# One pool of eight PSUM banks, four-bank score visits in segment 0, an exponential read from SBUF, and a new order

## The chip, the cores and the metric

The kernel runs on one core of one Trainium2 chip. The metric is the device time of one execution in microseconds. The core has TensorE (PE, with its weight loads shown as PEld), VectorE (DVE), ScalarE (ACT), GpSimd (POOL) and SyncE (SP), which here issues every DMA. PSUM has eight banks of 128 partitions by 512 fp32 values; matmuls write there, and DVE and ACT read it.

## The reference

A pre-norm layer on 2048 tokens of width 640: attention with a compressive memory, then a feed-forward network. Both halves are followed by a residual add.

```
h  = x + attention(layernorm(x))
h2 = h + feedforward(layernorm(h))

attention, 32 heads of width 20, 4 segments of 512 tokens, for each segment s:
    p      = softmax(causal(q k' / sqrt(20)));   a_dot = p v
    a_mem  = (phi(q) M) / (phi(q) z + 1e-6)      phi(t) = t + 1 if t > 0 else exp(t)
    o      = g a_mem + (1 - g) a_dot             g = sigmoid(beta), one per head
    M     += phi(k)' v;   z += sum phi(k)
    output = o wo
feedforward: silu(h w1) w2, inner width 1728
```

M and z start at zero, so segment 0 has no memory term.

## The kernel before, in words

The work is cut into named tasks (some 1,380), each with an engine, the tiles it reads and writes, and the code that emits its instructions. A string, `ORDER`, lists all tasks in one fixed order, found by a search outside the kernel with a model of costs. Each engine executes its own tasks in the order in which they stand there; between engines, semaphores that a tracker derives from reads and writes make an instruction wait. An entry such as `oe6x/A:0` names the task, for tasks that two engines can do the one chosen (A for ACT, D for DVE), and the buffer slots it takes. The numbers given to `G.task` as costs and priorities were of use to the search; in the emitted program only the order, the slots and the choice of engine count.

Names of tasks, with segment or tick numbers behind them:

- `n1_st`, `n1_rs`, `n1_ap`, `n1_tp`, `n1_te`, `n1_tr`: layernorm of a block of 128 tokens (statistics on DVE, root on POOL, apply on DVE) and its transpose, by matmul with an evacuation for segment 0 and by DMA afterwards. `n2_` is the same before the feed-forward network.
- `v`, `ve`: V projection (ten matmuls, L776) and its evacuation into Vx. `pr`: projection of q (last digit 0) or k (1) for a chunk of heads (five matmuls, L804); `qe`: the cast of its bank to QK (ACT L814 or DVE L815); `ex`: exp of it for phi (ACT L820); `ph`: the rest of phi on DVE (L827, L830). `re_`: rearrangement of the weights wq and wk.
- `qk`: a score visit, matmuls for a group of four heads (L877). The four heads are four row tiles of TensorE that write four banks. `e`: exp of two of those banks (ACT L888); `mk`: causal mask on POOL (L900).
- `av`: p v with four column tiles (L923); `oe`: evacuation into oTs (ACT L936, DVE L938); `tn`: transposes of it and the memory product (L952, L956); `nm`: division (DVE L969 to L989); `ad`: sum of both parts on POOL (L997).
- `kt`, `mz`, `ma`, `mb`: transpose of phi(k) by DMA, its product with V, and the update of Mz and its masked copy. `vt`: small DMAs that gather the heads 20 to 31 into QKV.
- `ot`, `wo`, `rs`: transpose of the attention's output by DMA (L1097), its product with wo (L1105), the residual add. `h1`, `th`, `s`: product with w1 (L1129), tanh on ACT (L1137), silu on DVE (L1143). `h2`, `o`, `out`: product with w2 (L1160), residual add (L1170), store.
- `w_...`, `x...`, `beta`: loads. The loads of wo, w1, w2 and the later x wait for a certain `nm` of segment 0. `fill31`: 31 matmuls on zeros into a free bank, whose result nobody reads.

Segment 0 has its groups in two halves of the queries: a tick x for the first 256 (score set `x`, 384 columns) and a tick y for the rest (sets `ya` of 512 columns and `yb` of 384). The segments 1 to 3 have one tick per group with sets `a`, `b` and, shared by two groups, `e`.

PSUM is two tensors of four banks: `ps_gen`, whose banks go to everything but scores (pool `ps`), and `ps_sc` for scores (pool `sc`). In segment 0 a score set is made in two visits of two banks each, in the other segments in one visit of four (`QUAD_SEGS`). An `ex` reads the projection's bank, as the `qe` does; reads of one bank by two engines are kept apart by the tracker, one behind the other.

The order interleaves the segments: while segment s is in its ticks, the projections of s + 1 and the feed-forward network of s - 1 are placed between the score visits. Behind the last score visit stand the last wo, h1 and h2 products.

Of the kernel before, what the change touches and what calls it, by code (L numbers as in the profile page):

```python
# [8 lines left out]
F32 = mybir.dt.float32  # L9
# [35 lines left out]
class Tracker:  # L45
# [29 lines left out]
    @staticmethod  # L75
    def _is_exclusive(key):
        return key[0] in ("ps", "sc")
# [133 lines left out]
class Alloc:  # L211
# [10 lines left out]
    def keys(self, subs):  # L222
        if self.pool in ("ps", "sc"):
            return [(self.pool, self.slot + i) for i in range(self.size)]
        return [(self.pool, self.slot, s) for s in subs]
# [99 lines left out]
D = 640  # L325
# [20 lines left out]
QUAD_SEGS = (1, 2, 3)  # L346
# [24 lines left out]
pr101:1 nm6x:0 e4ya0:1 e3yb2:1 av1y:0 oe0y/D:1 qk2yb0:2 e2yb0:0 qk2yb2:0 e2yb2 ex101:2 v12:2 qk3yb0:2 kt04:0 mta2
ot1:0 mm5 mk2yb ot0 w_w1_0 w_w1_2 e3yb0 w_w1_4 w_w1_1 oe1y/D:0 qe101/D:0 ph031:0 ve12/D qk2ya0:0 e2ya0:0 wo1:0 rs1
qk4ya2:2 qk2ya2:0 e2ya2 wo0:2 e4ya2 n2_st1:0 av2y:0 qk3ya0:0 e3ya0:0 qk3ya2:2 e3ya2 rs0 n2_st0:2 tn1y:1 pr120:2
qk4yb0:0 oe2y/D:0 tn2y:0 e4yb0:0 tn0y:3 qk4yb2:2 nm1y:0 n2_rs1 mk3yb mta0 mtb0 mm3 av3y:1 n2_rs0 e4yb2 n2_ap1:1
mk4yb nm0y:0 nm2y:1 qk5yb0:0 n2_ap0:0 qe120/D:0 mz00:3 mz04:0 ma00/D:1 e5yb0:1 oe3y/D:1 ph101:1 qk5ya2:2 ma04/D:2
ex120:0 e5ya2:0 qk5ya0:0 pr111:3 n2_tr1:0 qk5yb2:2 av4y:2 e5ya0 n2_tr0 qk6yb2:0 tn3y:0 h1_0_7_0:1 qe111/D:0 oe4y/D:0
tn4y:2 e5yb2 e6yb2:0 nm3y:1 ex111:2 nm4y:1 kt03:0 qk6ya0:2 x8:8,9,10,11 kt02:1 qk6yb0:0 ph111:0 ph120:0 h1_0_1_0:0
pr100:3 e6ya0:1 mk5yb mm6 e6yb0 mk6yb th0_7_0:0 ex100:0 qk6ya2:2 qk7yb0:0 e6ya2 qe100/D av5y:2 e7yb0:1 s0_7_0:0
h1_0_6_0:3 av6y:1 qk7ya0:2 oe5y/D:0 ph100:0 th0_1_0:0 th0_6_0:1 n1_st9:2 qk7yb2:0 e7yb2 e7ya0:1 s0_6_0 oe6y/D:1
s0_1_0 pr110:2 qk7ya2:0 tn6y:3 pr130:1 n1_st10:0 e7ya2 tn5y:0 nm6y:1 qk8a0:0 pr121:3 qe130/D:0 nm5y:1 ex110:0  # L380
ex130:2 e8a0:0 qe110/D e8a2 mz02:0 h1_0_11_0:1 th0_11_0:0 ex121:1 n1_st11:1 h1_0_5_0:2 th0_5_0:1 ma02/D:3 qe121/D
ph110:0 s0_11_0 vt16:0 w_w2_0:0 qk8b0:0 e8b2:0 e8b0 mm9 mzc3 mtb2 mzc9 mm4 mzc4 n1_rs9 mk7yb av7y:0 oe7y/D:0 mk8b
mm2 mm10 mm0 mzc6 s0_5_0 pr131:3 kt10:1 n1_st8:3 ex131:0 h1_0_2_0:1 tn7y:0 qk8e0:0 nm7y:1 th0_2_0:1 pr141:2 s0_2_0
h1_0_4_0:0 qe131/D h1_0_3_0:1 ph121:2 e8e0:1 e8e2 qk9a0:0 th0_4_0:1 th0_3_0:0 ot2 ot3 e9a2:1 e9a0 s0_4_0 ex141:1 mm7
n1_rs8 mm1 mzc1 mzc2 mzc10 mk8e mk8a mzc0 mzc5 n1_rs11 mz03:3 mm8 mb01:0 n1_rs10 mb00:0 mm11 mzc8 s0_3_0 h1_0_10_0:0
pr140:1 th0_10_0:0 ph130:0 qe141/D:0 ma03/D:4 qk9b0:0 wo2:2 n1_ap8:0 s0_10_0 e9b0:1 e9b2 av8:0 qe140/D n1_ap9:1 rs2
oe8/D:0 qk10a0:0 ex140:2 wo3:2 n2_st2:2 n1_ap10:2 e10a2:0 e10a0 h1_0_8_0:0 rs3 th0_8_0:0 qk10b0:0 e10b0:0 e10b2
# [24 lines left out]
ma22 tn19:2 nm19:1,0 e20b2:1 h2_2_2 mk20e e20b0 qk21a0:0 mk20b out3 n2_tr7 n2_tr6 e21a0:1 h2_2_3 e21a2 mk21a
h1_1_7_0:2 o2 ph240:0 mz14:3 th1_7_0:1 qk21b0:0 ma14 av20:0 out1 kt20:0 out2 x12 e21b0:0 e21b2 s1_7_0:0 oe20/D:1
# [38 lines left out]
def build(nc, es, A_x, A_wq, A_wk, A_wv, A_wo, A_beta, B_x, B_w1, B_w2, out):  # L452
# [118 lines left out]
    for b in range(4):  # L571
        load_x(b, 1, -100 + b)
# [660 lines left out]
```

## Time and profile before

| | us |
|---|---|
| median of three runs (330.74 to 332.19) | 331.64 |
| the profiled execution, its time | 331.8 |
| its span from first to last instruction | 330.1 |
| PE busy | 307.5 |
| PEld busy | 166.9 |
| DVE busy | 230.8 |
| ACT busy | 219.6 |
| POOL busy | 144.6 |

Busy time is the time in which an engine has at least one instruction in work; a matmul counts as busy for its whole way through the array, so short groups look longer than their columns. A view by stretches of time gives for each engine the busy time and, in brackets, the number of instructions, then the granted clock of TensorE (1.00 is full), the share of the DMA engines and GB/s. A row of the waits reads: who waited, for whom, us in total, times, the longest. A row of the timeline reads: start, duration, engine, line, operation, shapes, and in square brackets the idle time before it and what ended it. A row of the groups ends with the busy time and mean duration in ns, then the idle time before it.

### The profile page before, as it was taken

How to read it: one execution, taken by the hardware profiler on the slowest of the kernel's cores; microseconds unless marked ns; L12 is line 12 of the kernel's file. 1: busy time of each engine (PE TensorE's matmuls, PEld its weight loads, DVE VectorE, ACT ScalarE, POOL GpSimd, SP SyncE). 2: the span in 40 equal slices, each digit the busy share in tenths (PEclk: the TensorE clock that was granted, in tenths of full speed). 3: DMA queues.
4: the chain of work that ended last, by engine and by line, in shares of the span. 5: the costliest groups of instructions: out<-in, count | busy, mean ns of one | idle time of the engine just before them, and what ended most of it. 6: DMA issues, size and time to landing. Idle time of an engine off the chain costs nothing.

```text
span 330.1 us, 7228 instructions
## 1 busy us (share of the span) xinstructions
PE 307.5 (93%) x2874; PEld 166.9 (51%) x2874; DVE 230.8 (70%) x504; ACT 219.6 (67%) x306; POOL 144.6 (44%) x282
## 2 busy tenths in 40 slices
PE   8789798988897889998999999999999999999996
PEld 6534354444464544454654445545564446554563
DVE  5696847988898975876877985448866674855512
ACT  2659777998988798767776967776678880004400
POOL 3353861552958725273575434623576332120000
PEclk9999899999999999999999999999999999999999
DMA  7704376441744440006325030213441001350012
GB/s 209 251 0 76 71 200 180 131 97 16 165 85 86 114 108 2 1 23 107 68 66 133 24 71 10 18 33 68 93 91 34 0 2 21 60 119 2 0 40 101
DMA packets 48353, 24.56 MB, mean 74 GB/s; under 512 B 38848, under 2 KB 47232, under 8 KB 48320
## 3 DMA queue, kind: packets, MB, share of 16 engines
q1 hardware_dynamic: 48320, 24.10, 31.3%
q8 instruction: 23, 0.38, 0.5%
q14 instruction: 10, 0.08, 0.1%
HBM read 10.33 MB, written 2.62 MB: 39 GB/s over the span
## 4 chain that ended last, share of the span: by engine, by line
PE 56%; DVE 23%; ACT 7%; DMA 5%; SPq 5%; issue 3%; POOL 1%; DVEq 0%; ACTq 0%
PE ps_gen L1160 18%; PE ps_gen L1129 13%; PE ps_gen L804 6%; PE ps_sc L877 4%; PE ps_gen L923 4%; DVE stt L708 4%; PE ps_gen L1105 4%; DMA x_tok<-in_A_x_dram 4%; PE ps_gen L776 3%; DVE on L989 3%; DVE QK L815 2%; SPq L841 2%; ACT PTA L888 2%; ACT ex L820 2%; PE ps_gen L952 2%
## 5 line engine op out<-in xcount | busy, mean ns | idle before, releaser
L888 ACT ACTIVATE PTA<-ps_sc 128x1024 bf16<-128x1024 f32 x64 | 62.9, 1025 | 13.4 <-PE ps_sc L877 12.4
L1129 PE MATMUL ps_gen<-hT,w_sb 128*128 128x512 bf16 (+3 forms) x350 | 68.4, 338 | 2.5 <-DVE Vx L787 0.7
L900 POOL TENSOR_SCALAR_AFFINE_SELECT PTB<-PTB 128x512 bf16<-128x512 bf16 x64 | 40.9, 639 | 68.0 <-ACT PTB L888 65.8
L1160 PE MATMUL ps_gen<-w_sb,sT 128*128 128x320 bf16 x448 | 67.3, 300 | 0.6 <-DVE QK L815 0.2
L888 ACT ACTIVATE PTB<-ps_sc 128x1024 bf16<-128x1024 f32 (+1 forms) x64 | 59.9, 978 | 8.0 <-PE ps_sc L877 6.4
L1137 ACT ACTIVATE th<-ps_gen 128x512 f32<-128x512 f32 (+3 forms) x70 | 35.1, 520 | 39.6 <-PE ps_gen L1129 34.4
L1160 PEld LDWEIGHTS ps_gen<-w_sb,sT 128*128 128x128 bf16 x448 | 40.5, 98 | 24.1 <-issue 7.2
L1143 DVE SCALAR_TENSOR_TENSOR sT<-th,ps_gen 128x512 bf16<-128x512 f32 (+3 forms) x70 | 38.7, 570 | 16.4 <-ACT th L1137 15.9
L1129 PEld LDWEIGHTS ps_gen<-hT,w_sb 128*128 128x128 bf16 (+1 forms) x350 | 31.4, 98 | 31.7 <-issue 3.0
L888 ACT ACTIVATE PTE<-ps_sc 128x1024 bf16<-128x1024 f32 (+1 forms) x40 | 35.7, 938 | 6.3 <-PE ps_sc L877 5.2
L900 POOL TENSOR_SCALAR_AFFINE_SELECT PTE<-PTE 128x512 bf16<-128x512 bf16 x40 | 26.1, 651 | 14.3 <-ACT PTE L888 12.9
L708 DVE BATCH_NORM_STATS2 stt<-x_tok 128x6 f32<-128x320 bf16 x64 | 28.0, 480 | 3.1 <-DMA x_tok<-in_A_x_dram 3.0
L815 DVE CAST QK<-ps_gen 128x512 bf16<-128x512 f32 x31 | 21.0, 684 | 12.6 <-ACT ex L820 7.1
L1170 DVE SCALAR_TENSOR_TENSOR x_tok<-ps_gen,x_tok 128x640 bf16<-128x640 f32 x16 | 13.2, 824 | 23.2 <-PE ps_gen L1160 23.2
L776 PE MATMUL ps_gen<-wv_sb,xT 128*128 128x320 bf16 x160 | 25.3, 308 | 2.4 <-DMA wv_sb<-in_A_wv_dram 1.4
L1105 PE MATMUL ps_gen<-wo_sb,oT 128*128 128x320 bf16 x160 | 23.9, 299 | 3.5 <-DVE Mz L1070 1.2
L877 PE MATMUL ps_sc<-QK 20*128 20x256 bf16 (+3 forms) x360 | 24.1, 285 | 2.2 <-DVE QK L815 1.0
L938 DVE TENSOR_SCALAR oTs<-ps_gen,lsc 128x512 bf16<-128x512 f32 (+1 forms) x34 | 21.3, 628 | 6.8 <-PE ps_gen L923 6.8
L804 PE MATMUL ps_gen<-xT,wkr 128*128 128x512 bf16 x100 | 24.4, 380 | 1.2 <-DVE QK L815 0.6
L804 PE MATMUL ps_gen<-xT,wqr 128*128 128x512 bf16 x100 | 24.6, 380 | 0.8 <-DVE QK L815 0.8
L820 ACT ACTIVATE ex<-ps_gen 128x512 bf16<-128x512 f32 x30 | 18.1, 606 | 9.4 <-DVE QK L815 7.1
L900 POOL TENSOR_SCALAR_AFFINE_SELECT PTA<-PTA 128x512 bf16<-128x512 bf16 x24 | 15.6, 652 | 15.1 <-ACT PTA L888 15.1
(77 smaller groups left out, 401.3 us busy)
## 6 DMA issues: line engine op xcount, KB each, us to landing
out_dram<-x_tok SPq DMA_DIRECT2D x16, 160.0 KB, 2.0
w_sb<-in_B_w_dram SPq DMA_DIRECT2D x5, 432.0 KB, 5.9
x_tok<-in_A_x_dram SPq DMA_DIRECT2D x3, 640.0 KB, 4.8
w_sb<-in_B_w_dram SPq DMA_DIRECT2D x3, 640.0 KB, 5.0
QKV<-QK SPq DMA_DIRECT2D x16, 72.0 KB
wv_sb<-in_A_wv_dram SPq DMA_DIRECT2D x1, 800.0 KB, 6.9
sT<-in_A_wq_dram SPq DMA_DIRECT2D x1, 800.0 KB, 8.5
sT<-in_A_wk_dram SPq DMA_DIRECT2D x1, 800.0 KB, 10.3
```

What stands on the lines that cost most here:

```text
L708: T.add(DV, lambda e, hh=hh: e.bn_stats(out=stt[:, s, 6 * hh:6 * hh + 6], in_=xb[:, 320 * hh:320 * hh + 320]), reads=R((xa, xsub)), writes ...
L776: fns.append(lambda e, c=c, hh=hh: e.matmul(bank(ps, hh)[:, 0:320], lhsT=xT[:, c, 128 * i:128 * i + 128], rhs=wv_sb[:, c, 320 * hh:320 * h ...
L804: fns = [lambda e, kc=kc: e.matmul(bank(ps), lhsT=wt[:, kc, c, :], rhs=xT[:, kc, :], start=(kc == 0), stop=(kc == NC - 1)) for kc in range ...
L815: (lambda e: e.tensor_copy(out=o, in_=bank(ps)))
L877: fns.append(lambda e, j=j, o=o, r=r, q0=q0, q1=q1, qa=qa, ka=ka: e.matmul(sc_all[:, o:o + q1 - q0], lhsT=ka[32 * r:32 * r + DH, 128 * j:1 ...
L888: T.add(AC, lambda e: e.activation(out=pt[:, pta.slot, q0:q0 + 2, 0:width], in_=sc3[:, b0:b0 + 2, 0:width], func=ACT.Exp, scale=SCALE), re ...
L900: fns.append(lambda e, v=v: e.affine_select(out=v, in_=v, pattern=[[0, 4], [1, 128]], compare_op=ALU.is_ge, fill=0.0, base=0, channel_mult ...
L1105: fns.append(lambda e, c=c, hh=hh: e.matmul(bank(ps, hh)[:, 0:320], lhsT=oT[:, c, 128 * i:128 * i + 128], rhs=wo_sb[:, c, 320 * hh:320 * h ...
L1129: fns = [lambda e, c=c: e.matmul(bank(ps)[0:fw, lo:hi], lhsT=w1_sb[:, c, 128 * f:128 * f + fw], rhs=hT[:, c, lo:hi], start=(c == 0), stop= ...
L1137: T.add(AC, lambda e: e.activation(out=th[0:fw, tha.slot, lo:hi], in_=bank(ps)[0:fw, lo:hi], func=ACT.Tanh, scale=0.5), reads=R((ps, [0])) ...
L1143: T.add(DV, lambda e: e.scalar_tensor_tensor(out=sT[0:fw, f, lo:hi], in0=th[0:fw, tha.slot, lo:hi], scalar=1.0, in1=bank(ps)[0:fw, lo:hi], ...
L1160: fns.append(lambda e, f=f, fw=fw, hh=hh: e.matmul(bank(ps, hh)[:, 0:320], lhsT=sT[0:fw, f, 128 * i:128 * i + 128], rhs=w2_sb[0:fw, f, 320 ...
```

## The change

- One PSUM tensor of eight banks and one pool `ps` of eight slots serve everything, scores too. A score visit takes four neighbouring free banks.
- `QUAD_SEGS` includes segment 0: a set is one visit of eight matmuls and four banks, with two exps behind it as before. The 24 tasks for the second halves disappear.
- `ex` reads the bf16 cast in QK, not the bank, so it depends on the `qe` and no longer holds the bank.
- The `vt` copies of a segment use two semaphores instead of one.
- `ORDER` is new from the first entry to the last, with other slots and other choices of engine: of 40 `oe`, 15 are on ACT (6 before), of 40 `qe` 12 (9), of 16 `ve` 8 (6), of four `n1_te` 3 (2), of the five `ma` of segment 0 3 (0), of ten `re_` 4 (5). At the start 54 warm-up matmuls stand in one place, where 31 and 5 stood, and four and two more stand later, where two times two stood in segment 0.
- Several costs for the search are changed.

```diff
-        return key[0] in ("ps", "sc")
+        return key[0] == "ps"
...
-QUAD_SEGS = (1, 2, 3)
+QUAD_SEGS = (0, 1, 2, 3)
...
 ORDER = """
-zpad:0 x0:0 mt0 mt1 mt3 mta3 iota halfc epsc x1:1 x3:2 sel n1_st0:0 w_wv:0 n1_st1:1 n1_rs0 n1_ap0:0 fill31:0
-n1_tp0:0 n1_rs1 n1_ap1:1 x2:3 fill5:2 n1_tp1:2 n1_te0/A:0 n1_st3:0 n1_rs3 n1_st2:1 n1_te1/A epsg0 n1_rs2 w_q:0 v00:0
-n1_ap3:1 v01:2 ve00/A:0 n1_ap2:0 w_k n1_tp3:0 ve01/A re_wq0/A:0 n1_tp2:2 n1_te3/D v03:0 n1_te2/D pr000:2 re_wq2/A
...
+zpad:0 iota sel epsc x0:0 vpad0 mt2 x2:1 n1_st0:0 x1:2 x3:3 w_q:0 n1_st2:2 mta2 halfc mt0 mt1 n1_rs0 n1_st1:1
+n1_st3:3 epsg0 n1_ap0:0 n1_rs2 fill54:0 n1_tp0:0 n1_te0/A:0 n1_rs1 n1_rs3 n1_ap1:1 n1_ap2:2 n1_tp1:2 n1_te1/A
+n1_ap3:0 re_wq0/D:0 n1_tp2:4 n1_te2/D n1_tp3:6 n1_te3/A beta pr000:4 w_k zf0 re_wq1/A pr010:6 lsc0 re_wk0/D:0
+re_wk2/A pr001:5 re_wk1/D lsc1 mta1 lsc2 re_wk3/A qe000/D:0 pr011:7 w_wv:0 x4:4,5,6,7 qe001/A qe011/A:0 ex011:0 lsc3
+re_wq4/D re_wq2/D pr020:5 qk0x0:0 e0x2:0 e0x0 qe010/D pr031:7 pr021:6 qk1x0:0 vpad1 mtb1 mm5 mm1 mk0x n1_st5:3
...
+e7x0:0 mz02:4 e7x2 ma02/A:2 mk6x av6x:6 qk2yb0:0 mta0 mk7x e2yb2:1 e2yb0 mk2yb mtb0 tn5x:5 pr101:4 w_w2_1:0 w_w1_0:0
+w_wo:0 oe6x/D:1 av7x:6 nm5x:1 av1y:7 w_w1_3 oe7x/D:0 qk2ya0:0 ex100:1 tn6x:6 qe101/D e2ya2:0 e2ya0 nm6x:1 ex101:0
+pr130:5 tn7x:6 pr110:4 nm7x:1 qk3ya0:0 pr111:6 qe110/A:0 ph100:0 ph101:0 pr121:4 oe1y/D:0 ot0:0 qe111/D e3ya2:1
+e3ya0 qk3yb0:0 e3yb0:0 wo0:6 qe130/D:0 e3yb2 qe121/D:0 ex110:0 rs0 w_w1_1 ot1 mm0 mzc0 av2y:4 oe2y/A:1 n2_st0:3
...
+s2_11_0 h2_11_1 h2_8_0:4 h2_8_1 th2_13_0:1 ad31 s2_10_0 s2_13_0 ad30 ot15:0 wo15:0 rs15 ot14 n2_st15:2 wo14:2 ot12
...
-        "sT": 1, "th": 2, "st": 8, "const": 1, "ps": 4, "sc": 4,
+        "sT": 1, "th": 2, "st": 8, "const": 1, "ps": 8,
...
-    ps_all = es.enter_context(nc.psum_tensor("ps_gen", [128, 4 * 512], F32))
-    sc_all = es.enter_context(nc.psum_tensor("ps_sc", [128, 4 * 512], F32))
-    sc3 = sc_all[:, :].rearrange("p (b x) -> p b x", b=4)
+    ps_all = es.enter_context(nc.psum_tensor("ps_all", [128, 8 * 512], F32))
+    sc3 = ps_all[:, :].rearrange("p (b x) -> p b x", b=8)
...
-                    def e_ex(eng, ps=ps, exa=exa):
-                        T.add(AC, lambda e: e.activation(out=ex[:, exa.slot, :], in_=bank(ps), func=ACT.Exp),
-                              reads=R((ps, [0])), writes=R((exa, [0])))
+                    def e_ex(eng, c=c, w=w, exa=exa):
+                        T.add(AC, lambda e: e.activation(out=ex[:, exa.slot, :], in_=QK[:, c, w, :], func=ACT.Exp),
+                              reads=R((qk[c], [w])), writes=R((exa, [0])))
...
-        lane_v = T.lane(f"virt{s}")
+        lane_v = [T.lane(f"virt{s}a"), T.lane(f"virt{s}b")]
...
-                sca = G.alloc("sc", nr)
+                sca = G.alloc("ps", nr)
```

More of the change, by code (lines that the diff above doesn't have):

```diff
@@ L222, in keys @@
     def keys(self, subs):
-        if self.pool in ("ps", "sc"):
+        if self.pool == "ps":
             return [(self.pool, self.slot + i) for i in range(self.size)]
@@ L371 @@
[L371 to L375, printed above, removed]
```

208 lines of the change are left out of this document (102 added, 106 removed).

## The prediction

> **What bounds the kernel now.** I read the page first, then the busy time of each engine by stage, then the waits of ScalarE (ACT), then the timeline around single score visits. The page's engine totals:
>
> ```profile
> span 330.1 us, 7228 instructions
> PE 307.5 (93%) x2874; PEld 166.9 (51%) x2874; DVE 230.8 (70%) x504; ACT 219.6 (67%) x306; POOL 144.6 (44%) x282
> ```
>
> TensorE (PE) is busy for 93% of the span, VectorE (DVE) for 70%. An average hides where the rest lies, so the second view cuts the span at the first score visit, at the end of segment 0, and so on. A row has the stretch and its length in us, then the busy time (and instructions) of PE, PE's weight loads, DVE, ACT and POOL, the granted clock, and DMA:
>
> ```profile
> 0.00:18.50 18.50, 15.00 (x101) 10.00 (x101) 11.86 (x35) 8.61 (x18) 5.88 (x24) 1.00 0.64 205
> 18.50:78.60 60.10, 54.21 (x595) 26.83 (x595) 46.65 (x125) 49.19 (x73) 30.76 (x65) 0.97 0.42 104
> 78.60:150.00 71.40, 64.71 (x694) 35.73 (x694) 58.08 (x122) 60.26 (x85) 42.27 (x81) 1.00 0.33 72
> 150.00:205.00 55.00, 52.79 (x518) 28.14 (x515) 43.13 (x93) 41.86 (x55) 28.37 (x50) 1.00 0.34 69
> 205.00:272.00 67.00, 66.27 (x612) 34.34 (x610) 43.32 (x86) 51.15 (x65) 31.87 (x52) 1.00 0.22 42
> 272.00:330.00 58.00, 54.54 (x367) 31.89 (x364) 27.72 (x48) 8.57 (x15) 5.40 (x11) 1.00 0.19 49
> ...
> 60.00:90.00 30.00, 26.43 (x295) 14.24 (x293) 25.79 (x73) 27.98 (x43) 16.62 (x45) 1.00 0.41 88
> 90.00:120.00 30.00, 26.62 (x323) 15.71 (x326) 27.75 (x59) 25.06 (x35) 20.34 (x36) 1.00 0.51 113
> ```
>
> From 205 us on TensorE has nothing left to give: 66.27 of 67.00 us. Its idle time lies before: 5.9, 6.7 and 2.2 us in the three stages from 18.5 to 205 us, 14.8 us together, and 3.5 us in the startup. The last two rows say why: from 60 to 90 us ACT is busy 27.98 of 30 us, from 90 to 120 us DVE 27.75 of 30. There TensorE waits for whichever of the two is full, while the other has 2 to 5 us spare. So time comes back only if matmul slots are saved, if banks come free earlier, or if ACT and DVE are loaded more evenly before 205 us.
>
> **The change, part by part.**
>
> Four-bank visits in segment 0. Its 24 score sets are now made in one visit of eight matmuls, not two of four; matmuls, columns and exponentials are the same. A two-bank visit and a four-bank one in the timeline, each with the row after it:
>
> ```profile
> 59.69 0.34 PE L877 MATMUL ps_sc<-QK 20*128 20x256 bf16 x4
> 59.96 0.22 PE L956 MATMUL ps_gen<-ident,oTs 128*128 128x96 bf16 x1
> ...
> 78.59 0.40 PE L877 MATMUL ps_sc<-QK 20*128 20x384 bf16 x8 [0.32 <-ACT PTA L888]
> 78.92 0.29 PE L923 MATMUL ps_gen<-PTA,Vx 128*32 128x256 bf16 x4
> ```
>
> From start to next start the small visit takes 0.27 us and the large one 0.33. A set goes from 0.54 to 0.33 us, and 24 sets save 5.0 us of matmul slots. All lie in a stage where TensorE is idle 10% of the time and ACT is nearly as full, so I count half: **-2.5 us** (0 to -5.0).
>
> The other side of it: two small visits let TensorE fill one pair of banks while ACT empties the other. A large visit holds four, and in the new order the next one nearly always uses the same four, so ACT stands between them unless other work is queued there. ACT's waits, first in segment 0 (18 to 78 us), then in the rest (78 to 272 us), where the visits already are large:
>
> ```profile
> ACT PTA L888 <- PE ps_sc L877: 2.8, 6, 1.4
> ACT PTB L888 <- PE ps_sc L877: 2.7, 4, 1.6
> ACT PTE L888 <- PE ps_sc L877: 0.3, 1, 0.3
> ...
> ACT PTA L888 <- PE ps_sc L877: 9.6, 11, 1.4
> ACT PTE L888 <- PE ps_sc L877: 4.9, 7, 2.0
> ACT PTB L888 <- PE ps_sc L877: 3.7, 8, 0.7
> ```
>
> That is 5.8 us in segment 0 now. The 60 large visits later cost 18.2 us, 0.30 each; 24 of them would cost 7.2, 1.4 more. ACT is busy 49.19 of 60.10 us (0.82) in this stage, so I take 0.82 x 1.4 = **+1.1 us** (0 to +8.0; the upper end is the second rival).
>
> Exponential of the feature map from SBUF. Today the cast of q or k (DVE or ACT) and the exponential (ACT) both read the projection's bank, one after the other, and the bank is free only after both. Who waited for the exponential, and what it costs beside ACT's reads of SBUF at line 689:
>
> ```profile
>   DVE QK L815: 7.1, 8
>   PE ps_gen L1105: 0.8, 1
>   PEld ps_gen L1129: 0.8, 2
>   PEld ps_gen L804: 0.5, 1
>   PE ps_gen L804: 0.3, 1
> ...
> L820 ACT ACTIVATE ex<-ps_gen 128x512 bf16<-128x512 f32 x30 | 18.1, 606 | 9.4 <-DVE QK L815 7.1 <-DVE phiK L830 1.4 <-PE ps_gen L804 0.5
> L689 ACT ACTIVATE wkr<-sT 128x400 bf16<-128x400 bf16 x3 | 1.6, 525 | 0.0
> L689 ACT ACTIVATE wkr<-sT 128x80 bf16<-128x80 bf16 x2 | 0.5, 258 | 0.0
> ```
>
> DVE no longer waits for it (7.1 us). TensorE's own waits on it are 2.4 us with the weight loads, 1.1 without; I take **-1.5 us** (0 to -2.4). The exponential must now follow the cast in every case, where ACT could go first before: it already waits 7.1 us for casts, and the next user, the phi pair on DVE, comes much later in the order, so I cost this at nothing; without that cover it is one cast of 0.7 us per late pair. As to its duration, 80 to 400 elements from SBUF give 0.834 ns per element, so 512 take 618 ns against 606 from PSUM: 30 x 12 ns = 0.4 us of ACT, hidden in its waits.
>
> The Trainium skill ("VectorE: DVE Perf Modes", section on the TRN2 errata) speaks against this part: a ScalarE instruction pays a fixed 224 cycles when it reads SBUF and 172 when it reads PSUM. By that the 30 exponentials would cost 30 x 43 ns = 1.3 us more, an estimate from that page, and this part would come to -0.2 us instead of -1.5 if all of it showed.
>
> One pool of eight banks. Reading the slots in the new order: score visits stay on banks 0 to 3 through most of segment 0, use 4 to 7 for four visits early in it, and move there for good in segment 1. In effect these are two halves of four that swap three times; only startup and the last segment's h1 and h2 use all eight. Nothing waits there now (54.54 of 58.00 us busy, the rest being the last residual and store), so 0 us (bounds 0 and -0.7, the idle time of the stage before).
>
> The new order and the engine choices in it. Counting the names, nine oTs evacuations, three casts, two V evacuations, one xT evacuation and three copies to Mz go from DVE to ACT, one weight rearrangement the other way. With the rows
>
> ```profile
> L938 DVE TENSOR_SCALAR oTs<-ps_gen,lsc 128x512 bf16<-128x512 f32 (+1 forms) x34 | 21.3, 628 | 6.8 <-PE ps_gen L923 6.8
> L936 ACT ACTIVATE oTs<-ps_gen,lsc 128x512 bf16<-128x512 f32 (+1 forms) x6 | 3.9, 652 | 1.0 <-PE ps_gen L923 1.0
> L815 DVE CAST QK<-ps_gen 128x512 bf16<-128x512 f32 x31 | 21.0, 684 | 12.6 <-ACT ex L820 7.1 <-PE ps_gen L804 5.6
> L814 ACT ACTIVATE QK<-ps_gen 128x512 bf16<-128x512 f32 x9 | 5.4, 597 | 4.0 <-PE ps_gen L804 4.0
> ```
>
> the evacuations alone are 9 x 0.628 + 3 x 0.684 = 7.7 us off DVE and 9 x 0.652 + 3 x 0.597 = 7.7 us onto ACT; with the smaller ones, about 10 us each way. What evening out can bring is bounded by the two rows from 60 to 120 us: ACT and DVE together fill 53.8 and 52.8 of 60 us, so with both full the same work takes 3.1 and 3.6 us less, 6.7 us. The other stages have slack in both, and there I add nothing. I take three quarters, **-5.0 us**. The ends: all idle TensorE time from 18.5 to 205 us but the 1.1% that remains after 205 (-12.8), and half of the moved 10 us showing up on ACT (+5).
>
> Startup. The four x blocks are loaded before any weight, then wq, beta, wk, wv; 54 warm-up matmuls replace 36; q and k projections go ahead of v. The first score visit starts at 18.51 us now. It should come 1 to 2 us earlier, but the v products (2.88 us for two blocks) are then still owed: 0 us (-2 to +2).
>
> ```profile
> 9.17 2.88 PE L776 MATMUL ps_gen<-wv_sb,xT 128*128 128x320 bf16 x20 [1.37 <-DMA wv_sb<-in_A_wv_dram]
> 18.51 0.35 PE L877 MATMUL ps_sc<-QK 20*128 20x256 bf16 x8
> ```
>
> SP's queue. Four weight loads (w2_1, w1_0, wo, w1_3, 2.3 MB) now stand directly ahead of the first transpose of otok, which wo0 needs; before, only wo and w1_3 were ahead of a transpose there, and it landed late (first the 15 transposes of phiK, then the one at 44 us behind those two loads):
>
> ```profile
> phiKt<-phiK SPq DMA_TRANSPOSE x15, 2.6
> ...
> phiKt<-phiK SPq DMA_TRANSPOSE x1, 5.1
> ```
>
> 1.2 MB cost 2.5 us more; 2.3 MB would cost about 5. Eleven groups of matmuls stand between the loads and wo0 in the order, four projections among them, so most of it is covered; I take **+1 us** (0 to +5, nothing covered). The two semaphores for the QKV copies, the planner's cost numbers and the names are free.
>
> Sum: -2.5 + 1.1 - 1.5 - 5.0 + 0 + 1 = -6.9 us on the profiled execution, whose time was 331.8 us (span 330.1, 1.7 us around it) and which lies 0.2 us above the median of 331.64: **324.9 us**.
>
> **The rivals.**
>
> *The order does much more.* If the new order brings TensorE's idle share before 205 us to the share after it, 12.8 us go, and half the visits' 5.0: 331.8 - 15.3 = 316.5. For it: ACT and DVE are not full after 120 us. Against: the q, k, v products of a segment need the previous stage's evacuations.
>
> *Slower: ACT stands between the large visits.* If each of the 24 costs ACT what one late visit cost on average when it did wait (18.2 us in 26 waits, 0.70 each), that is 16.8 instead of 5.8 us, 0.82 of it on the path: +9.0; evening out then brings nothing, since ACT is the full engine, and the rest (-2.5 - 1.5 + 1) stays: 331.8 + 6.0 = 337.8. It decides from 0.39 us per visit on (24 x 0.39 - 5.8, times 0.82, is the 3.0 us that stay). Against it: 0.30 us on average now, and in the new order other ACT work lies in most of the gaps.
>
> *No change.* The 10 us moved onto ACT cost there what DVE gains, and the three small terms cancel: about 331.5.
>
> *The clock drops more often in segment 0.* The two pairs of filler matmuls there are gone.
>
> ```profile
> 40.00:50.00 10.00, 9.88 (x117) 4.83 (x109) 5.43 (x16) 7.49 (x11) 6.04 (x11) 0.86 0.67 181
> ...
> 40.74 2.56 PE L776 MATMUL ps_gen<-wv_sb,xT 128*128 128x320 bf16 x10
> 45.63 1.52 PE L776 MATMUL ps_gen<-wv_sb,xT 128*128 128x320 bf16 x10
> ```
>
> The granted clock was 0.86 from 40 to 50 us, and ten matmuls took 2.56 us instead of 1.52. A mean of 0.86 is 2.8 us at half clock, 1.4 us lost; two more such drops give 324.9 + 2.8 = 327.7. The Trainium skill ("TensorE: Matmul & The Clock Gate", part 1) says that an idle window of about 3.4 us halves the clock; the trace agrees in size (2.8 us at half clock), but not in the cause: the row has TensorE busy for 9.88 of the 10 us.
>
> **How the numbers follow.** Forecast 0.41 (its own range 321 to 329: the small terms' ends), much more 0.17, clock 0.10, no change 0.15, slower 0.17. A change under 0.5% (1.7 us) can't be told from none here. Faster: 0.41 + 0.17 + 0.10 = 0.68; same 0.15; slower 0.17. The range goes from just under 316.5 to 334, which leaves out the worst part of the slower case and a little below.
>
> **What would show it.** Right: score visits of eight matmuls at 0.33 us in segment 0; the exponential at 610 to 650 ns and no DVE wait on it; DVE near 220 us and ACT near 230 busy; TensorE idle from 18.5 to 205 us near 8 us. The new order puts 25 more h1 matmuls behind the last score exponential, which ends at 271.28 us now, so it must end near 257. Wrong: ACT waiting over 0.39 us per visit in segment 0, a wait at wo0 on the transpose of several us, or a last exponential after 265 us.
>
> ```profile
> 270.26 1.02 ACT L888 ACTIVATE PTB<-ps_sc 128x1024 bf16<-128x1024 f32 x1
> ```

## The result and the profile after

The changed kernel takes 319.49 us (median of 4 runs, 317.07 to 321.78) beside 331.47 us before in the same session: ratio 0.964, 95% interval 0.956 to 0.972. Run again later with six runs it came to 318.94 us, ratio 0.960 (0.956 to 0.964). The forecast was 324.9 us: the right sign, and 12.0 us gained where 6.9 were forecast.

The page of the changed kernel (profiled execution 318.7 us):

```profile
span 317.0 us, 7256 instructions
PE 301.8 (95%) x2894; PEld 167.6 (53%) x2894; DVE 220.7 (70%) x488; ACT 226.6 (71%) x322; POOL 145.1 (46%) x282
```

Start with a subtraction. Busy TensorE time fell from 307.5 to 301.8 us, which is 5.7. Idle TensorE time fell from 22.6 (330.1 - 307.5) to 15.2 us, which is 7.4. Together they are the 13.1 us between the two spans. DVE lost 10.1 us of work, as forecast; ACT took on 7.0, where about 10 were forecast.

Where the idle time went shows in the busy time by stage, cut as in the prediction (stretch, length, then PE, PE's weight loads, DVE, ACT, POOL, granted clock, DMA):

```profile
0.00:18.50 18.50, 15.69 (x111) 10.02 (x112) 14.07 (x40) 8.25 (x17) 8.00 (x31) 1.00 0.64 205
18.50:78.60 60.10, 56.43 (x634) 31.11 (x635) 42.78 (x113) 53.68 (x86) 28.72 (x62) 0.97 0.61 144
78.60:150.00 71.40, 68.70 (x764) 39.47 (x761) 53.82 (x120) 65.41 (x92) 43.91 (x78) 1.00 0.27 49
150.00:205.00 55.00, 52.39 (x500) 26.22 (x499) 42.43 (x90) 45.71 (x61) 30.13 (x54) 1.00 0.28 57
205.00:272.00 67.00, 66.75 (x643) 37.54 (x641) 48.71 (x96) 45.38 (x57) 32.76 (x54) 1.00 0.27 47
272.00:316.90 44.90, 41.86 (x254) 23.27 (x252) 18.93 (x32) 8.19 (x14) 1.57 (x4) 1.00 0.18 52
```

From 18.5 to 205 us TensorE now idles 9.0 us instead of 14.8, and the saving lies in the first two stages (5.9 to 3.7, 6.7 to 2.7). ACT does 53.68 and 65.41 us of work there instead of 49.19 and 60.26: the same clock, and more work on TensorE and ACT at once (DVE has less, by what moved to ACT). The third stage has not gained.

Where the busy time went shows in the score matmuls from 17.5 to 82 us, nearly all of them of segment 0; first before, then after:

```profile
L877 PE MATMUL ps_sc<-QK 20*128 20x256 bf16 (+3 forms) x136 | 10.1, 260 | 1.8 <-DVE QK L815 1.0 <-ACT PTE L888 0.3 <-ACT PTA L888 0.3
L877 PE MATMUL ps_sc<-QKV 20*128 20x256 bf16 (+1 forms) x72 | 5.6, 266 | 1.3 <-DMA QKV<-QK 0.7 <-ACT PTE L888 0.5
```

```profile
L874 PE MATMUL ps_all<-QK 20*128 20x256 bf16 (+3 forms) x132 | 6.4, 266 | 1.2 <-DVE oTs L935 0.9 <-ACT PTE L885 0.2
L874 PE MATMUL ps_all<-QKV 20*128 20x256 bf16 (+1 forms) x72 | 3.3, 255 | 0.1
```

A single matmul lasts as long as before (about 260 ns), and there are nearly as many. But the group's busy time fell from 15.7 to 9.7 us, because eight of them in a row overlap more than four and four. These 6.0 us count overlap with the neighbouring matmuls too. If each matmul is counted only up to the start of the next one, the 192 score matmuls of segment 0 took 12.4 us before and take 7.5 now: 4.8 us of the 5.7 by which TensorE's busy time fell. Counted in the same way, the warm-up matmuls (60 instead of 40) add 1.7 us, and all other groups together save 2.5.

Now the places that the prediction named, in the changed kernel. ACT's waits on score matmuls from 17.5 to 82 us (sum, times, longest):

```profile
ACT PTB L885 <- PE ps_all L874: 1.7, 4, 0.6
ACT PTA L885 <- PE ps_all L874: 1.3, 2, 0.8
ACT PTE L885 <- PE ps_all L874: 1.0, 2, 0.6
```

The exponential of the feature map among the groups (busy, mean ns, idle before it):

```profile
L817 ACT ACTIVATE ex<-QK 128x512 bf16<-128x512 bf16 x30 | 19.0, 636 | 0.0
```

TensorE's waits at the wo matmuls, which need the transposes of otok:

```profile
PE ps_all L1102 <- DMA oT<-otok: 1.5, 3, 0.9
```

And from the timelines the first score visit and the last score exponentials:

```profile
17.44 0.34 PE L874 MATMUL ps_all<-QK 20*128 20x256 bf16 x8
...
251.34 1.94 ACT L885 ACTIVATE PTA<-ps_all 128x1024 bf16<-128x1024 f32 x2 [0.16 <-PE ps_all L874]
```

ACT waits 4.0 us for scores in this stage instead of 5.8, and it never stands idle ahead of an exponential of the feature map (9.4 us before). One thing the prediction had not looked for: these exponentials have been postponed. Matching each with its projection in the trace, it starts 17.1 us after the projection's last matmul on average (2.0 us before the change). That needs the SBUF source: in the new order there are 26 places at which a projection's bank is given away before its exponential has run.

### The profile page after: what moved, and what is told of

The parts are those of the page before. It is cut to its first block, busy times and chain, and to the rows that moved or that the text cites. A ratio compares the mean times of both kernels' runs of the same rounds, so it can differ in the third digit from the quotient of the medians.

```text
span 317.0 us, 7256 instructions
## 1 busy us (share of the span) xinstructions
PE 301.8 (95%) x2894; PEld 167.6 (53%) x2894; DVE 220.7 (70%) x488; ACT 226.6 (71%) x322; POOL 145.1 (46%) x282
## 3 DMA queue, kind: packets, MB, share of 16 engines
HBM read 10.33 MB, written 2.62 MB: 41 GB/s over the span
## 4 chain that ended last, share of the span: by engine, by line
PE 71%; DVE 9%; ACT 8%; DMA 7%; SPq 2%; issue 1%; POOL 1%; DVEq 0%; ACTq 0%
PE ps_all L1157 19%; PE ps_all L1126 18%; PE ps_all L801 10%; PE ps_all L874 6%; PE ps_all L773 5%; PE ps_all L1102 5%; PE ps_all L920 4%; DMA sT<-in_A_wk_dram 3%; ACT PTE L885 3%; DMA oT<-otok 2%; ACT PTA L885 2%; PE ps_all L949 2%; ACT PTB L885 2%; PE ps_all L953 1%; DVE on L986 1%
## 5 line engine op out<-in xcount | busy, mean ns | idle before, releaser
L1126 PE MATMUL ps_all<-hT,w_sb 128*128 128x512 bf16 (+3 forms) x350 | 67.6, 337 | 1.1 <-DMA hT<-xn_rot 0.6
L885 ACT ACTIVATE PTA<-ps_all 128x1024 bf16<-128x1024 f32 x64 | 62.4, 1026 | 8.3 <-PE ps_all L874 7.3
L1157 PE MATMUL ps_all<-w_sb,sT 128*128 128x320 bf16 x448 | 67.2, 300 | 0.4 <-DVE on L986 0.3
L885 ACT ACTIVATE PTB<-ps_all 128x1024 bf16<-128x1024 f32 (+1 forms) x64 | 58.9, 970 | 8.3 <-PE ps_all L874 8.1
L1134 ACT ACTIVATE th<-ps_all 128x512 f32<-128x512 f32 (+2 forms) x70 | 34.5, 522 | 33.2 <-PE ps_all L1126 29.0
L1140 DVE SCALAR_TENSOR_TENSOR sT<-th,ps_all 128x512 bf16<-128x512 f32 (+2 forms) x70 | 38.8, 575 | 22.2 <-ACT th L1134 21.4
L1157 PEld LDWEIGHTS ps_all<-w_sb,sT 128*128 128x128 bf16 x448 | 40.7, 98 | 24.1 <-issue 7.2
L1126 PEld LDWEIGHTS ps_all<-hT,w_sb 128*128 128x128 bf16 (+1 forms) x350 | 31.6, 98 | 29.6 <-issue 5.4
L885 ACT ACTIVATE PTE<-ps_all 128x1024 bf16<-128x1024 f32 (+1 forms) x40 | 35.9, 944 | 5.1 <-PE ps_all L874 4.6
L773 PE MATMUL ps_all<-wv_sb,xT 128*128 128x320 bf16 x160 | 25.5, 310 | 0.1
L994 POOL TENSOR_TENSOR otok<-on 128x320 bf16<-128x320 bf16 x24 | 19.1, 798 | 10.8 <-DVE on L986 10.6
```

What stands on the lines that cost most here:

```text
L773: fns.append(lambda e, c=c, hh=hh: e.matmul(bank(ps, hh)[:, 0:320], lhsT=xT[:, c, 128 * i:128 * i + 128], rhs=wv_sb[:, c, 320 * hh:320 * h ...
L885: T.add(AC, lambda e: e.activation(out=pt[:, pta.slot, q0:q0 + 2, 0:width], in_=sc3[:, b0:b0 + 2, 0:width], func=ACT.Exp, scale=SCALE), re ...
L994: T.add(PO, lambda e: e.tensor_tensor(out=o_dst, in0=on[:, ona.slot, 0, :].rearrange("p (i x) -> p i x", i=4), in1=on[:, ona.slot, 1, :].r ...
L1126: fns = [lambda e, c=c: e.matmul(bank(ps)[0:fw, lo:hi], lhsT=w1_sb[:, c, 128 * f:128 * f + fw], rhs=hT[:, c, lo:hi], start=(c == 0), stop= ...
L1134: T.add(AC, lambda e: e.activation(out=th[0:fw, tha.slot, lo:hi], in_=bank(ps)[0:fw, lo:hi], func=ACT.Tanh, scale=0.5), reads=R((ps, [0])) ...
L1140: T.add(DV, lambda e: e.scalar_tensor_tensor(out=sT[0:fw, f, lo:hi], in0=th[0:fw, tha.slot, lo:hi], scalar=1.0, in1=bank(ps)[0:fw, lo:hi], ...
```

## The experiments

All times below are medians beside the kernel before on the same chip. The runs were spread over three chips, so they are compared by their ratios; the changed kernel stands at 0.960.

**1. Two-bank visits in segment 0 of the changed kernel.**

```diff
-QUAD_SEGS = (0, 1, 2, 3)
+QUAD_SEGS = (1, 2, 3)
-... qk5yb0:0 qe120/A qe140/D ...
+... qk5yb0:0 qk5yb2:2 qe120/A qe140/D ...
```

> The changed kernel with one part undone: segment 0 goes back to two-bank score visits, each four-bank set cut into two visits at the same place in the order. All else stays: pool of eight, exp from SBUF, new order. My theory (the gain sits in the order, which pulls matmul work forward and puts the exps of the feature map off): the 24 extra visits cost what the prediction gave them, 0.1 us each, so 322 us (319.5 to 324.5). Rival 'the visits are the gain', by the sum of start-to-start waits of the visits of segment 0, which fell from 14.6 to 9.0 us: 325 us or more. Rival 'ACT stands between large visits': undoing them helps, 317 to 319 us, and ACT's waits on score matmuls fall below 4.0 us in 17 to 82 us.

Measured: 318.70 us, ratio 0.959 (0.956 to 0.963): no difference. My 322 us was too high. The rival that undoing the large visits helps names 317 to 319 us, but the ratio is the changed kernel's, and ACT's waits for scores from 17 to 82 us are 4.2 us, not below 4.0. The timeline at a former large visit, and the score matmuls from 17.5 to 82 us, say why:

```profile
58.90 0.35 PE L874 MATMUL ps_all<-QK 20*128 20x256 bf16 x8
59.17 0.40 PE L920 MATMUL ps_all<-PTA,Vx 128*32 128x256 bf16 x8
```

```profile
L874 PE MATMUL ps_all<-QK 20*128 20x256 bf16 (+3 forms) x128 | 6.8, 259 | 0.8 <-DVE oTs L935 0.5 <-ACT PTE L885 0.2
L874 PE MATMUL ps_all<-QKV 20*128 20x256 bf16 (+1 forms) x72 | 3.3, 255 | 0.0
```

Two visits that stand next to each other run as one row of eight, 0.27 us to the next start, and the group is busy for 10.1 us, like the changed kernel's 9.7. In the order before, the halves of a set stood 2 to 130 entries apart. So in the new order four banks in one visit are worth nothing by themselves; by the trace, what saves TensorE time is that the halves stand together. Neither a run that pulls them apart in the new order was made, nor one that joins them in the old, so how much of the 12 us this is, I read from the trace and have not shown alone.

**2. The same, with the first-needed half ahead.** In 16 of the 24 sets the half that ACT empties first now also comes first on TensorE.

```diff
-... qk5yb0:0 qk5yb2:2 ...
+... qk5yb2:2 qk5yb0:0 ...
```

> The changed kernel with two-bank visits in segment 0, and in the 16 of its 24 sets whose second exp stands first in ACT's queue the two visits exchanged, so that ACT's first exp of the set waits for two banks of matmuls instead of four. Theory 'ACT standing between visits costs something in segment 0': ACT's wait for score matmuls in 17 to 82 us falls below 3 us (4.0 in the changed kernel) and the time to 316 to 318 us. Rival 'this wait hides behind matmul work that PE has in any case': 318 to 320 us, as with four-bank visits.

Measured: 319.35 us, ratio 0.960 (0.957 to 0.963). ACT's waits for scores from 17 to 82 us are 4.0 us, as they were, so the exchange did not do what it was made for, and what these waits cost is not settled by it. The changed kernel itself, run beside it:

> The changed kernel itself, as the common measure for the three beside it: 318 to 320 us.

Measured: 318.94 us. None of the variants beats it.

**3. The engine choices of before, in the new order.** 51 tasks change engine, 34 of them from ACT to DVE.

```diff
-... qe120/A ... oe8/A ... ve11/A ...
+... qe120/D ... oe8/D ... ve11/D ...
```

> The changed kernel with the order kept, but with the engine choices (ACT or DVE) of the kernel before for the 51 tasks that stand in both and differ. My theory: an even split of ACT and DVE is not what brought the gain, so 319 to 322 us. Rival 'the engine choices are the gain' (the prediction's bound for evening ACT and DVE out was 6.7 us): 324 to 326 us.

Measured: 342.90 us, ratio 1.033 (1.029 to 1.038): 24 us slower than the changed kernel, and slower than the old. My theory missed, and the rival's 324 to 326 us too. In the rows of ACT's score exponentials, the idle time ahead of them (third column) rose from 8.3 + 8.3 + 5.1 to 44.9 us:

```profile
L883 ACT ACTIVATE PTA<-ps_all 128x1024 bf16<-128x1024 f32 x64 | 62.4, 1024 | 19.5 <-PE ps_all L872 16.7 <-PE ps_all L918 1.6 <-POOL PTB L895 0.9
L883 ACT ACTIVATE PTB<-ps_all 128x1024 bf16<-128x1024 f32 (+1 forms) x64 | 59.0, 970 | 17.7 <-PE ps_all L872 17.4
L883 ACT ACTIVATE PTE<-ps_all 128x1024 bf16<-128x1024 f32 (+1 forms) x40 | 35.7, 943 | 7.7 <-PE ps_all L872 7.6
```

**4. The engine choices of after, in the old order.**

```diff
-... qe120/D ... oe8/D ...
+... qe120/A ... oe8/A ...
```

> The kernel before in its own order, with the engine choices (ACT or DVE) of the changed kernel for the 51 tasks that differ. Theory 'engine choices fit only the order that they were chosen with' (undoing them in the changed kernel cost 23 us): slower than before, 334 to 350 us. Rival 'the new choices even ACT and DVE out and gain by themselves': 322 to 328 us.

Measured: 350.30 us, ratio 1.050 (1.045 to 1.055). So the same 51 choices cost 17 us in the one order and save 24 in the other. They have no worth of their own; a list names the engine and the place together.

**5. The exponentials early, from SBUF.** Each of the 30 stands directly behind its eviction.

```diff
-"ex": 3
+"ex": 8
-qe121/D:0 ex110:0 rs0 ...            (ex121 some 230 entries later)
+qe121/D:0 ex121:3 rs0 ...
```

> The changed kernel with each of the 30 exps of the feature map put directly behind the eviction of its projection in the order (in the changed kernel they start 17.1 us after the projection on average, before the change 2.0 us), still reading SBUF; eight buffers for their results instead of three, everything else as in the changed kernel. My theory: postponing them is a large part of what the order gains, because 0.64 us of ACT work then stands ahead of score exps that TensorE waits for: 323 to 327 us, with more PE idle before 140 us. Rival 'only the source of the exp matters, not its place': 319 to 320 us.

**6. The exponentials early, from the bank.**

```diff
-out=ex[:, exa.slot, :], in_=QK[:, c, w, :]
+out=ex[:, exa.slot, :], in_=bank(ps)
```

> As the kernel with early exps, but each exp reads the PSUM bank of its projection, as before the change. My theory: the bank is freed by the exp instead of by the eviction, some 0.6 us later, and an exp costs 606 instead of 636 ns; both are small, so within 2 us of the kernel with early exps from SBUF. Rival 'the gain is the bank that comes free earlier': 3 us or more slower than the early exps from SBUF. Rival 'the 30 ns are what counts': 1 us faster than those.

**7. The exponentials some 20 entries behind the eviction (18 on average, at most 24), from SBUF.**

```diff
-qe121/D:0 ex110:0 rs0 w_w1_1 ...
+qe121/D:0 rs0 w_w1_1 ... n2_st1:1 w_w2_0 ex121:3 ...
```

> The changed kernel with the exps of the feature map at most 20 entries behind the eviction instead of 79 on average (directly behind cost 16 us), from SBUF, eight result buffers. Theory 'head of the queue': what cost 16 us was ACT standing for DVE's eviction (10.8 us), so with that wait below 2 us the time is 319 to 322 us. Rival 'work in the way': 0.64 us of ACT work ahead of score exps costs wherever ACT is full, so 325 to 333 us although ACT no longer waits for the eviction, with PE's waits for the exps of the scores far above the changed kernel's 1.2 us.

Measured: 335.74 us (1.011, 1.008 to 1.014), 346.26 us (1.043, 1.039 to 1.048) and 322.68 us (0.972, 0.967 to 0.976). Against the changed kernel's ratio of 0.960 these are 17, 28 and 4 us. For the three in turn, the exponential's row among the groups of ACT, and below it TensorE's waits on ACT. Directly behind the eviction, from SBUF:

```profile
L816 ACT ACTIVATE ex<-QK 128x512 bf16<-128x512 bf16 x30 | 18.8, 630 | 11.2 <-DVE QK L811 10.8
```

```profile
PE ps_all L873 <- ACT PTA L884: 5.7, 6, 2.2
PE ps_all L873 <- ACT PTB L884: 4.5, 7, 1.4
PE ps_all L873 <- ACT PTE L884: 3.0, 3, 2.2
```

Directly behind it, from the bank:

```profile
L816 ACT ACTIVATE ex<-ps_all 128x512 bf16<-128x512 f32 x30 | 17.9, 600 | 15.4 <-DVE QK L811 15.0
```

```profile
PE ps_all L1125 <- ACT ex L816: 6.4, 4, 2.5
PE ps_all L919 <- ACT ex L816: 3.3, 5, 1.3
PE ps_all L772 <- ACT ex L816: 2.7, 2, 1.9
```

Some 20 entries behind it, from SBUF (this profile is of the slowest of the six executions, 326.0 us):

```profile
L815 ACT ACTIVATE ex<-QK 128x512 bf16<-128x512 bf16 x30 | 18.4, 630 | 0.0
```

```profile
PE ps_all L872 <- ACT PTA L883: 3.0, 4, 1.4
PE ps_all L872 <- ACT PTB L883: 1.2, 4, 0.6
```

Directly behind the eviction, ACT stands 10.8 us for DVE, the score exponentials queue behind that, and TensorE waits for score banks to be emptied (13.2 us; 1.2 in the changed kernel). Some twenty entries later ACT waits for nothing ahead of them (0.0), and of the 17 us some 4 are left. So about 13 us go together with the wait at the head of ACT's queue. That the other 4 are the exponentials' work in the way of the scores fits TensorE's waits (4.2 us instead of 1.2), but no run separates it. The Trainium skill ("PSUM — Partial Sum Buffer", section "Engine vs sequencer instructions") says that ScalarE's queue is strict first in, first out. The 10.8 us agree with it.

The bank costs 10.5 us more, where I had expected under 2: h1, attention and v matmuls wait 12.4 us for banks that the exponential still holds. Not all of the 10.5 us need be waiting: TensorE is also busy for 309.8 us instead of 302.7, at a mean granted clock of 0.975 instead of 0.995. Even so, the SBUF source carries the new order: not by its price (630 against 600 ns) but by letting the exponential be late without holding a bank.

**8. The exponential from SBUF in the old order.**

```diff
-ex031:0 qe041/D:0 ... qe031/D lsc3
+qe041/D:0 ... qe031/D ex031:0 lsc3
```

> The kernel before with one part of the change: the exp of the feature map reads SBUF, with the 15 exps that stood ahead of their projection's eviction moved directly behind it; the order is otherwise the old one. My theory after the early exps (an exp directly behind the eviction makes ACT wait for DVE, 7.1 us in the kernel before, 10.8 us with early exps in the changed one): no gain from the source alone, 331 to 335 us, and ACT's wait for the eviction stays at 7 us or more. The prediction's term for this part, banks free 0.6 us earlier, would give 330 us.

Measured: 332.62 us, ratio 1.002 (0.998 to 1.005): nothing, as expected.

```profile
L819 ACT ACTIVATE ex<-QK 128x512 bf16<-128x512 bf16 x30 | 18.7, 630 | 13.1 <-DVE QK L814 12.9
```

ACT's wait for evictions rose from 7.1 to 12.9 us. TensorE's waits for score banks rose with it, first before, then here:

```profile
PE ps_sc L877 <- ACT PTE L888: 0.8, 2, 0.5
PE ps_sc L877 <- ACT PTA L888: 0.6, 2, 0.3
```

```profile
PE ps_sc L876 <- ACT PTB L887: 2.5, 6, 1.5
PE ps_sc L876 <- ACT PTA L887: 1.7, 4, 0.9
PE ps_sc L876 <- ACT PTE L887: 1.5, 2, 1.2
```

That is 4.3 us more. On the other side DVE's 7.1 us of waiting for the exponential are gone, and so are TensorE's own waits on it. Gain and cost balance: the run shows that the source by itself brings nothing in the old order, not that the longer wait was free.

**9. The exponentials postponed in the old order.**

```diff
-qe031/D ex031:0 lsc3 ...
+qe031/D lsc3 ... mk6x ex031:1 mtb1
```

> The kernel before, exp from SBUF, and the exps postponed in the old order: up to 80 entries behind the eviction, at least 12 ahead of the feature map where that is possible (mean 37 entries; 79 in the changed kernel, 0 before). Theory 'the postponed exps are worth their waits by themselves': ACT's wait for the eviction falls from 7.1 to below 3 us and the time to 324 to 328 us. Rival 'postponing pays only in an order made for it': 329 to 333 us, the wait gone from the exps but found again at the score exps or the matmuls.

Measured: 336.62 us, ratio 1.009 (1.005 to 1.013), slightly slower. The first theory's time is out, but the run does not settle why: of the 30 exponentials, eight still stood next to their evictions, because their feature map follows at once, and ACT's wait only came down to 8.5 us, not below 3.

**10. Feed-forward work not pulled forward.**

```diff
-e8a0:0 mk7yb e8a2 h2_0_0:6 n1_st10:3 ...
+e8a0:0 mk7yb e8a2 n1_st10:3 ... ad14 nm15:0,1 h2_0_0:0 e16a0 ...
```

> The changed kernel with one piece of the order undone: the second feed-forward matmuls of token blocks 0 and 1 (h2_0 and h2_1, 9.4 us of PE work, at 80 to 90 us in the changed kernel, after 135 us before the change) stand directly around those of block 2 again, with what follows them on DVE and the output DMAs. Theory 'the order gains by having matmul work that waits for nobody in the stages where ACT and DVE set the pace': PE idles more than 2.7 us in 82 to 150 us and the time is 322 to 327 us. Rival 'the places of these matmuls do not matter, PE works them off later all the same': 318 to 320 us.

Measured: 332.97 us, ratio 1.002 (0.999 to 1.005): 14 us slower than the changed kernel, and back at the time before. TensorE at 80 us, first in the changed kernel, then here (start, duration, line; in brackets the idle time before):

```profile
81.59 0.40 PE L874 MATMUL ps_all<-QK 20*128 20x384 bf16 x8
81.92 2.99 PE L1157 MATMUL ps_all<-w_sb,sT 128*128 128x320 bf16 x20
84.85 0.40 PE L874 MATMUL ps_all<-QK 20*128 20x256 bf16 x8
85.18 1.26 PE L1157 MATMUL ps_all<-w_sb,sT 128*128 128x320 bf16 x8
```

```profile
79.98 0.40 PE L872 MATMUL ps_all<-QK 20*128 20x384 bf16 x8
83.00 0.61 PE L872 MATMUL ps_all<-QK 20*128 20x256 bf16 x8 [2.62 <-ACT PTB L883]
85.67 0.61 PE L872 MATMUL ps_all<-QK 20*128 20x512 bf16 x4 [1.62 <-ACT PTE L883]
```

In the changed kernel the h2 matmuls (line 1157) fill the time in which ACT empties the score banks. Without them TensorE stands, and then the clock goes as well:

```profile
78.10:81.50 3.40, 1.30 (x28) 0.51 (x25) 3.29 (x11) 3.11 (x5) 1.48 (x4) 1.00 0.04 8
82.00:96.00 14.00, 9.74 (x78) 4.82 (x79) 7.46 (x21) 10.84 (x15) 7.41 (x15) 0.53 0.51 77
```

From 82 to 96 us the granted clock is 0.53 (1.00 in the changed kernel). How much of the 14 us is waiting and how much is the clock, the run does not tell apart; the matmuls that were moved take only 8.7 us themselves in the changed kernel (not the 9.4 that I had expected).

**11. No shared pool until the last visit.**

```diff
-... s0_8_1 v23:0 e14a2:0 ... qk16a0:4 pr230:3
+... s0_9_1 v23:4 qk14b0:0 ... qk16a0:0 pr230:7
```

> The changed kernel with the pool of eight given up as long as score visits are left: visits use banks 0 to 3 only, all other tiles 4 to 7; after the last visit all eight are free for all as in the changed kernel. Five tiles (pr030, v03, wo0, v23, tn22) wait for a bank and stand 1 to 16 entries later, the rest keeps its place. My theory (the pool is hardly used across the halves while visits are left): 318 to 321 us. Rival 'one pool carries the new order': 323 us or more, with PE waiting for banks at these tiles.

Measured: 345.45 us, ratio 1.040 (1.036 to 1.043), 26 us slower. But this is no clean test of the pool. Besides the five delayed tiles, of the 223 tiles other than scores that are placed before the last visit 152 start in another bank of their half than in the changed kernel. TensorE's largest wait is for banks of h1 tiles, far from the five:

```profile
PE ps_all L1124 <- DVE sT L1138: 6.4, 8, 2.1
```

So which of several free banks a tile takes is probably worth a lot in an in-order list, but the run changes both, banks and delays. What the pool itself is worth stays open.

## Why the prediction was right, and where it fell short

The measured 319.49 us lie inside the stated range, but below the forecast's own 321 to 329, and nearer to the rival "the order does much more" (316.5) than to 324.9. The direction and the place of the gain were right; the division into terms was not.

- *Reading of the bound: right.* It placed the recoverable time between 18.5 and 205 us and forecast some 8 us of idle TensorE time left there; 9.0 were. That this is so close is partly luck: 8 is 14.8 less the whole 6.9, and so takes the visits' saving off the idle time, where it came off the busy time. DVE near 220 us and ACT near 230 us came out at 220.7 and 226.6, the exponential at 636 ns lay within 610 to 650, and the last score exponential ended at 253.3 us (251.34 + 1.94; near 257 forecast).
- *Four-bank visits, -2.5: mis-sized.* The step "so I count half" failed. By the trace the score matmuls of segment 0 take 4.8 us less of TensorE's time, nearly the full 5.0. My reading is that with other matmul work pulled into the gaps, TensorE is 95% busy, and a saved slot is hardly lost in waiting; no run shows this term alone. The cause was also named too narrowly: the two halves need to stand together, not to share a visit (run 1).
- *ACT standing between visits, +1.1: did not come.* ACT waits 4.0 us in segment 0, less than the 5.8 before and not 7.2, with four-bank visits as with two-bank ones (runs 1 and 2). The rival built on it needed 0.39 us per visit; it was 4.0 / 24 = 0.17.
- *Exponential from SBUF, -1.5: wrong as a gain of its own* (run 8: +0.5 us, -0.6 to +1.5). In the changed kernel DVE's casts no longer wait for it (its phi waits 2.0 us), and TensorE's waits on it fell to 0.5 us, from 2.9 (the prediction's 2.4 left out two rows of 0.3 and 0.2). But the step "I cost this at nothing" failed: in run 8 ACT waits 5.8 us more for casts, and TensorE 4.3 us more for score banks. In the new order, directly behind the eviction, 10.8 us of such waits go with 13 us of time (runs 5 and 7). What the source brings is the freedom to run late without a bank, and that sits in the order. As to its price, 30 ns more were measured (636 against 606). They lie between the 12 worked out from rows and the 43 estimated from the Trainium skill ("VectorE: DVE Perf Modes", section on the TRN2 errata). That the -1.5 and the +1.1, neither of which came, nearly cancel in the sum is luck.
- *The order, -5.0: right in kind, too small, and bounded by the wrong quantity.* With the visits taken out, the other terms came to -4.4 (-5.0 - 1.5 + 1.1 + 1); the idle time fell by 7.4. The bound of 6.7 us was ACT's and DVE's unevenness. But the engine choices are no gain by themselves: put into the old order they cost 17 us (run 4), and the new order, chosen together with them, takes 24 us longer without them (run 3). What the new order does is put matmul work that waits for nobody beside ACT's work (run 10) and move ACT work that nobody waits for out of the way (runs 5 to 7). The rival "the order does much more" is nearest in time, but by a sum that is not this one: it has about 2 us of TensorE's time idle from 18.5 to 205 us, and 9.0 were.
- *Pool, 0:* open (run 11). *Startup, 0:* the first visit comes at 17.44 instead of 18.51 us, idle time in the startup falls from 3.5 to 2.8. *SP's queue, +1:* 1.5 us of waits at the wo matmuls. *Clock:* 0.97 in segment 0 before and after, so that rival did not come in this change; run 10 shows what it looks like when it does.

The undone pieces cost 14, 17 and 24 us, each more than the 12 us of the whole change. They are not shares of the gain: each breaks a list in which every place was chosen with the others. They show what the gain depends on. Some of these costs include a lower clock: in the profiled executions TensorE's mean granted clock is 0.995 in the changed kernel and in run 5, but 0.989, 0.980, 0.975, 0.979 and 0.975 in runs 3, 4, 6, 10 and 11. How much that adds was not separated.

## What to carry to other kernels

With strictly ordered queues, an engine choice or an operand's source has no price apart from the order: the same 51 engine choices cost 17 us in one order and save 24 in the other, and a source that brings nothing in the old order is needed in the new. Look for two things in the stage where an off-path engine sets the pace: long matmul work that waits for nothing to put beside it, and work nobody waits for that stands at the head of its queue. And before halving a saved slot "because the engine idles there", ask whether the same change fills those gaps.

## What the runs showed of the hardware

- The granted clock can halve after a stretch that is not wholly idle. In run 10 it drops at 81.5 us. In the 3.40 us ahead of that TensorE was busy for 1.30 us (38%), with no pause over 1.2 us in them: the pause of 2.62 us begins at 80.38 us and ends behind the drop. It then ran at half clock for some 13.6 us, to about 95 us. The Trainium skill ("TensorE: Matmul & The Clock Gate", part 1) gives at least one idle window of about 3.4 us as the condition. The half clock agrees; a wholly idle window was not needed here. In the prediction I put the drop before down to no idleness, since TensorE was busy for 9.88 of the 10 us from 40 us on. But that drop came at 39.45 us, and in the 3.40 us ahead of it TensorE was busy for 2.22. After the change it comes at 35.14 us, behind 2.01 of 3.40. Each of these two lasted 3.4 us. First before, then after:

```profile
36.05:39.45 3.40, 2.22 (x32) 1.03 (x32) 3.19 (x10) 2.60 (x4) 3.19 (x7) 1.00 0.37 71
```

```profile
31.70:35.10 3.40, 2.01 (x52) 1.20 (x51) 2.24 (x7) 3.40 (x5) 2.05 (x5) 1.00 0.49 94
```

- The busy share in the profile alone does not decide it. The changed kernel kept the full clock behind the first stretch below (57% busy, 37 steps of 3.41 us after the drop at 35.14 us), while run 9 lost it directly behind the second (78% busy; 0.50 from 41.4 us on). What decides stays open.

```profile
161.40:164.80 3.40, 1.93 (x31) 1.03 (x31) 3.25 (x10) 2.90 (x4) 1.46 (x3) 1.00 0.83 134
```

```profile
37.95:41.35 3.40, 2.64 (x42) 1.11 (x39) 2.56 (x7) 2.98 (x4) 1.93 (x4) 1.00 0.64 132
```

- A long DMA issue on SP at the start goes with its place in the queue, not with the transfer. The issue of beta took 2.87 us before, as the eighth, and 0.52 us now that it is the sixth; the stall has moved to the x blocks, now the ninth. First before, then after:

```profile
4.27 2.87 SPq L577 DMA_DIRECT2D beta_bc<-in_A_beta_dram  x1
```

```profile
3.15 0.52 SPq L574 DMA_DIRECT2D beta_bc<-in_A_beta_dram  x1
...
4.76 1.88 SPq L562 DMA_DIRECT2D x_tok<-in_A_x_dram  x1
```
